# Converting the last four weight chunks in the first layer's first two steps, in half chunks, instead of beside attention

## The chip, the cores and the metric

The kernel runs on one core of a Trainium2 chip, as one launch. The metric is the device time of one execution in microseconds (us). The engines are named as the profile names them: PE is TensorE's matmul, PEld its weight load, DVE is VectorE, ACT is ScalarE, POOL is GpSimd, SP is SyncE, whose queue issues nearly all DMAs here.

## The reference

```python
# attention: 8 batches, 8 heads, 576 tokens, head size 64
scores = scale * np.matmul(q, k.transpose(0, 1, 3, 2))
thresh = np.max(scores, axis=-1, keepdims=True) - tau
scores = np.where(scores >= thresh, scores, -1000000000.0)
attn = np.exp(scores - np.max(scores, axis=-1, keepdims=True))
attn = attn / (np.sum(attn, axis=-1, keepdims=True) + 1e-09)
x = np.matmul(attn, v)                  # then (B,H,S,D) -> (4608 tokens, 512)
# feed-forward
h = np.maximum(x @ w_in, 0.0)           # w_in: 512 x 2048
out = (h * h) @ w_out                   # w_out: 2048 x 512
```

[...]

## The kernel before, in words

**Three stages.** Attention runs in 72 periods, each with two units of 128 queries for two heads. Then come two layers of the feed-forward, each over nine steps of 512 tokens (NSTEP = 9): the first, `hidden_layer`, gives g = relu(x @ w_in)^2, and the second, `output_layer`, gives g @ w_out. Both layers use a two-level fast matrix product that takes seven products where the plain one takes eight, so a step is 7 groups (m in OUTER = 1, 2, 6, 7, 4, 5, 3) of 7 products, 49 products. A product of the first layer is four 128x128 by 128x128 matmuls into one PSUM bank (line 825). The price is sums: of the weights, of x (`prepare_x`, line 774), and of the results.

**A group of the first layer** (`inner`, line 702) makes its products in the order 1, 6, 7, 5, 2, 4, 3 into four banks X, Y, Z, W: X, Y, Z and W get the first four, and X, Z and W are used once more, each accumulating onto what is there. ScalarE copies X out (L737), and VectorE reads Y, Z, W, X, Z, W in that order with an addition each (L125). The sixth product (onto Z) can't begin before VectorE has read the first Z, the seventh (onto W) not before it has read the first W. After each product comes a tick, `also(m, at)`, which issues side work: `convert_out` and `chain_out` first, then in groups three to six (ticks 14 to 40) the sums for the next step's x, `sum_v`, with a ScalarE copy into PSUM (L771) and a VectorE addition (L122). ScalarE also squares finished blocks (L804, L805), and GpSimd makes the rest of the result's sums (L125 on POOL).

**Order.** Everything is under a manual schedule: each engine runs its instructions in the order in which the program issues them, and so does SP's queue with its DMAs.

**The conversion of a weight chunk** (128x512 numbers) has six parts: ScalarE takes the high words' magnitude (`convert1`, L205); GpSimd scales the low words (`convert2`, L212), clamps (`convert3`, L219) and at the end adds (`convert6`, L245); VectorE shifts and merges (`convert4`, L227, and `convert5`, L235). There are 16 chunks of w_in and 16 of w_out. EARLY says how many of w_out's are done beside attention, one chunk started per period: `starts` holds the periods 2 to 33, and a period p is a converting one if p or p - 1 is in `starts`. Such a period uses the order CONVERTING, any other the order PLAIN. In CONVERTING the two reads of the attention output (`values_out`) are ScalarE copies and GpSimd multiplies; in PLAIN they are VectorE multiplies (L644). From the first plain period on, GpSimd also makes the sums of w_in (`sums_step`, at most two in a period before period 60).

**The path of this change.** `convert_out` (line 1057) is called at every tick of the first layer and works on `halves_`, the half chunks of the w_out blocks that are not early, PER = 4 in a step. With EARLY = 16 the list is empty and it does nothing. Converted w_out blocks go to DRAM, where `chain_out` reads them for w_out's own sums; the blocks that stand last in the list are first read there in the third step.

Of the kernel before, what the change touches and what calls it, by code (L numbers as in the profile page):

```python
# [12 lines left out]
U32 = mybir.dt.uint32  # L13
ALU = mybir.AluOpType
AF = mybir.ActivationFunctionType
# [33 lines left out]
def kernel(  # L49
# [25 lines left out]
    nc = tc.nc  # L75
# [82 lines left out]
    def raw_at(m):  # L158
        return RAW.index(m)
# [1 line left out]
    def made_at(m):  # L161
        return 4 + MADE.index(m) if m in MADE else RAW.index(m)

    EARLY = 16
    chunks, out_blocks = [], {}
    for r, c, m_, k_ in blocks(AT_B):
        out_blocks[m_, k_] = moe_w_out[ds(r * BANK, BANK), ts(c, P)].rearrange("(k p) o -> p k o", p=P)
# [2 lines left out]
    blocks_out = [(m, k) for k in RAW for m in RAW]  # L170
    chunks += [(W_OUT, m, k, out_blocks[m, k]) for m, k in blocks_out[:EARLY]]
    is_wide = moe_w_in.dtype != FP32
# [24 lines left out]
    def pick(t, k):  # L197
        return t.rearrange("p (n two) -> p n two", two=2)[:, :, k]
# [7 lines left out]
        parts[m] = (lo, hi, a)  # L206
        raws.pop(m)

    def convert2(m):
        if m in parts:  # L210
            lo = parts[m][0]
            nc.gpsimd.tensor_scalar(out=lo, in0=lo.bitcast(U32), scalar1=2.0**-29, scalar2=None, op0=ALU.mult)  # L212

    def convert3(m):
        if m not in parts:
# [7 lines left out]
    def convert4(m):  # L223
        if m not in parts:
            return
        lo, hi, a = parts[m]
        nc.vector.tensor_scalar(  # L227
            out=a, in0=a, scalar1=3, scalar2=0x3FFFFFFF, op0=ALU.logical_shift_left, op1=ALU.bitwise_and
        )

    def convert5(m):
        if m not in parts:
            return
        lo, hi, a = parts[m]
        nc.vector.scalar_tensor_tensor(  # L235
            out=hi, in0=hi, scalar=-(1 << 30), in1=a, op0=ALU.bitwise_and, op1=ALU.bitwise_or
        )
# [323 lines left out]

    starts = {m + 2: m for m in range(16 + EARLY)}
    X_FIRST = 40
# [44 lines left out]
    def period(p):  # L608
# [63 lines left out]
        def every(key):  # L672
# [7 lines left out]
            "SA": scored_a, "SB": scored_b,  # L680
            "PV": PV, "x": values_out, "xm": given_out,
            "c1": lambda: convert1(begun(p)), "c2": lambda: convert2(begun(p)),
            "c3": lambda: convert3(begun(p)), "c4": lambda: convert4(begun(p - 1)),
            "c5": lambda: convert5(begun(p - 1)), "c6": lambda: convert6(begun(p - 1)),
# [317 lines left out]
    with tc.manual_schedule():  # L1002
# [45 lines left out]
        chain_at, over_at = 26 * BANK, 26 * BANK + 2 * BANK  # L1048
        halves_ = [(m, k, h) for m, k in blocks_out[EARLY:] for h in range(2)]
        chains = [((0, RAW.index(k)), c) for k in RAW for c in range(4)]  # L1050
# [6 lines left out]
        def convert_out(n, tick):  # L1057

            base = X_AT[(n + 1) % 2] + 7 * BANK
            mine = list(enumerate(halves_))[PER * n : PER * (n + 1)]  # L1060
            for j, (i, (m, k, h)) in enumerate(mine):
                place = w_slots[:, raw_at(m), raw_at(k), ds(h * BANK // 2, BANK // 2)]
                raw = arena[:, ds(base + j * BANK, BANK)]
                own = (base - 4 * BANK, base + 4 * BANK, base + 4 * BANK + BANK // 2, over_at)
                a = arena[:, ds(own[j], BANK // 2)]
                key, step = ("out", i), tick - BEGIN - 2 * j
                if tick == 0:
                    src = out_blocks[m, k][:, 2 * h : 2 * h + 2, :]
                    if not is_wide:
                        nc.sync.dma_start(out=two(raw[:, 0 : BANK // 2]), in_=src)  # L1070
                        nc.sync.dma_start(out=place, in_=raw[:, 0 : BANK // 2])
                        continue
                    nc.sync.dma_start(out=two(raw.bitcast(I32)), in_=src.bitcast(I32))
                if not is_wide:
                    continue
                lo, hi = pick(raw.bitcast(I32), 0), pick(raw.bitcast(I32), 1)
                if step == 0:
                    b = b_pool.tile([P, BANK], FP32, tag="b", name="cw")[:, 0 : BANK // 2]
                    nc.scalar.activation(out=b, in_=hi.bitcast(FP32), func=AF.Abs)
                    parts[key] = (lo, hi, b.bitcast(I32))  # L1080
                    convert2(key)
                if step == 2:
                    low, high = (0x38000000, 0x47EFFFFF)
                    b = parts[key][2].bitcast(FP32)
                    nc.vector.tensor_scalar(
                        out=b, in0=b, scalar1=as_float(high), scalar2=as_float(low), op0=ALU.min, op1=ALU.max
                    )
                    convert4(key)
                    convert5(key)
                if step == 5:  # L1090
                    parts.pop(key)
                    nc.gpsimd.tensor_tensor(out=a.bitcast(I32), in0=hi, in1=lo, op=ALU.add)
                if step == 6:
                    nc.sync.dma_start(out=place, in_=a)
# [22 lines left out]
        for n in range(NSTEP):  # L1117
# [15 lines left out]
            def also(m, at):  # L1133
                i = OUTER.index(m)
                convert_out(n, 7 * i + at)
                chain_out(n, 7 * i + at)
                if not last:
                    if 2 <= i <= 5 and at < 6:
                        next(xsums)
                    return  # L1140
                spread(work.get(i, []), at)
                if 7 * i + at > 9:
                    reload(7 * i + at - 10)
# [46 lines left out]
def as_float(bits):  # L1190
    import struct

    return struct.unpack("<f", struct.pack("<I", bits))[0]
# [30 lines left out]
```

## Time and profile before

| | |
|---|---|
| time, median of 3 runs | 1308.91 us (1307.8 to 1309.66) |
| time of the profiled execution | 1308.12 us |
| its span, first to last instruction | 1306.3 us |
| attention (before the first matmul of L825) | 0 to 512.3 us |
| first layer (L825) | 512.3 to 906.5 us |
| second layer (L960) | 906.5 to 1306.3 us |
| busy, share of the span | PE 98%, DVE 77%, POOL 70%, ACT 65% |
| mean granted TensorE clock | 0.998 |

In lines of groups the columns are: line, engine, operation, out<-in, shapes, count, then busy us and mean ns of one, then the engine's idle time before them and what ended it. In lines by windows they are: stretch, its length, busy us of PE, PEld, DVE, ACT and POOL with the number of instructions, granted clock, share of the DMA engines, GB/s. In lines of the timeline they are: start, length, engine, line, operation, count, and in brackets the idle time before.

### The profile page before, as it was taken

The page shows a single profiled execution, that of the slowest core. Times are in us where ns is not written, and L with a number is a line of the kernel's source. Part 1 is how long each engine was busy: PE and PEld are TensorE (multiplying, and loading weights), DVE is VectorE, ACT ScalarE, POOL GpSimd, SP SyncE. Part 2 cuts the span into 40 slices and gives each one's busy share as a digit, 9 for nine tenths or more (in the row PEclk, how much of TensorE's full clock was granted, in tenths as well). Part 3 has the DMA queues.
Part 4 walks back from the last instruction along what each step waited for, and adds up shares of the span by engine and source line. Part 5 has one row for each costly group of instructions (what it writes and reads, how often), then busy time and mean ns, then how long its engine had stood idle before and what let it go on. Part 6 is the DMA issues. An engine that isn't in the chain of part 4 may idle for free.

```text
span 1306.3 us, 47872 instructions
## 1 busy us (share of the span) xinstructions
PE 1284.5 (98%) x19483; PEld 1159.8 (89%) x19483; DVE 1010.8 (77%) x2431; ACT 845.7 (65%) x1498; POOL 916.4 (70%) x1023
## 2 busy tenths in 40 slices
PE   8999999999999999999999999999999999999998
PEld 5777777677777777999999999999999999999998
DVE  5999999999999996877787778777646654665463
ACT  5999999888898985657665766675523432433240
POOL 2777778755555320978897789768777777777775
PEclk9999999999999999999999999999999999999999
DMA  6565666544333313466556665569645234522511
GB/s 153 145 160 140 169 182 188 147 103 104 89 78 79 79 41 80 133 200 218 182 181 194 203 208 164 180 247 393 245 158 162 63 105 158 162 68 96 162 34 33
DMA packets 247035, 192.12 MB, mean 147 GB/s; under 512 B 97184, under 2 KB 195488, under 8 KB 246816
## 3 DMA queue, kind: packets, MB, share of 16 engines
q1 hardware_dynamic: 245504, 188.66, 48.5%
q8 instruction: 153, 2.51, 0.8%
q14 instruction: 66, 0.54, 0.2%
q10 hardware_dynamic: 1312, 0.41, 0.1%
HBM read 116.65 MB, written 72.35 MB: 145 GB/s over the span
## 4 chain that ended last, share of the span: by engine, by line
PE 87%; ACT 5%; DMA 3%; DVE 3%; issue 1%; POOL 1%; SPq 0%; ACTq 0%; DVEq 0%; POOLq 0%
PE po L960 29%; PE ph L825 28%; PE sc L532 11%; PE sc L434 10%; PE pt L380 5%; DVE arena L452 3%; ACT arena L462 2%; PE sc L515 2%; DMA wall<-w 2%; PE sc L398 2%; ACT arena L523 1%; PE sc L380 1%; DMA g<-arena 1%; ACT arena L403 0%; ACT c L771 0%
## 5 line engine op out<-in xcount | busy, mean ns | idle before, releaser
L125 POOL TENSOR_TENSOR arena<-arena 128x512 f32<-128x512 f32 (+1 forms) x314 | 378.1, 1223 | 129.1 <-DVE arena L125 115.1
L960 PE MATMUL po<-wall,arena 128*128 128x128 f32 x3528 | 394.7, 275 | 1.4 <-ACT arena L737 1.4
L960 PEld LDWEIGHTS po<-wall,arena 128*128 128x128 f32 x3528 | 394.3, 192 | 1.8 <-ACT arena L737 1.8
L825 PE MATMUL ph<-arena,wall 128*128 128x128 f32 x3528 | 394.2, 275 | 0.7 <-DVE arena L644 0.7
L825 PEld LDWEIGHTS ph<-arena,wall 128*128 128x128 f32 x3528 | 394.0, 192 | 0.8 <-issue 0.8
L125 DVE TENSOR_TENSOR arena<-ph,arena 128x512 f32<-128x512 f32 x378 | 256.3, 688 | 86.3 <-PE ph L825 63.2
L122 POOL TENSOR_TENSOR arena<-arena 128x128 f32<-128x128 f32 (+2 forms) x314 | 255.4, 814 | 53.8 <-DMA arena<-w 37.6
L125 DVE TENSOR_TENSOR arena<-po,arena 128x128 f32<-128x128 f32 x378 | 108.4, 290 | 168.6 <-PE po L960 164.5
L467 DVE SCALAR_TENSOR_TENSOR arena<-arena 128x576 f32<-128x576 f32 x288 | 237.4, 860 | 1.3 <-POOL arena L459 0.8
L452 DVE TENSOR_SCALAR_CACHE_REDUCE arena<-sc 128x576 f32<-128x576 f32 x288 | 205.0, 747 | 14.6 <-ACT arena L523 4.8
L462 ACT ACTIVATE arena<-arena 128x576 f32<-128x576 f32 x288 | 208.1, 773 | 11.8 <-DVE arena L452 8.5
L771 ACT COPY c<-arena 128x512 f32<-128x512 f32 (+1 forms) x303 | 173.5, 579 | 49.6 <-DVE arena L122 41.7
L532 PEld LDWEIGHTS sc<-arena 64*64 64x64 f32 x5760 | 159.2, 133 | 36.7 <-DVE arena L452 20.2
L532 PE MATMUL sc<-arena 64*64 64x128 f32 (+1 forms) x5760 | 180.8, 262 | 2.7 <-DVE arena L452 1.3
L434 PE MATMUL sc<-arena 64*64 64x64 f32 (+1 forms) x2304 | 176.9, 414 | 6.2 <-ACT arena L403 4.2
L122 DVE TENSOR_TENSOR arena<-arena,c 128x512 f32<-128x512 f32 (+1 forms) x267 | 174.9, 663 | 5.5 <-ACT c L771 4.0
L523 ACT COPY arena<-pt 128x1024 f32<-128x1024 f32 x144 | 146.4, 1017 | 30.5 <-PE pt L380 29.4
L737 ACT COPY arena<-po 128x128 f32<-128x128 f32 x63 | 16.6, 264 | 186.7 <-PE po L960 184.0
L380 PEld LDWEIGHTS pt<-ident,arena 64*128 64x128 f32 x2304 | 83.4, 139 | 39.4 <-ACT arena L523 30.1
L737 ACT COPY arena<-ph 128x512 f32<-128x512 f32 x63 | 36.6, 581 | 123.1 <-PE ph L825 122.5
L434 PEld LDWEIGHTS sc<-arena 64*64 64x64 f32 x2304 | 74.3, 134 | 45.1 <-ACT arena L403 15.1
L380 PE MATMUL pt<-ident,arena 64*128 64x64 f32 x2304 | 102.2, 228 | 2.3 <-ACT arena L523 2.3
(50 smaller groups left out, 922.2 us busy)
## 6 DMA issues: line engine op xcount, KB each, us to landing
g<-arena SPq DMA_DIRECT2D x144, 256.0 KB, 2.6
arena<-g SPq DMA_DIRECT2D x144, 256.0 KB, 4.6
w<-arena SPq DMA_DIRECT2D x60, 256.0 KB, 2.4
wall<-w SPq DMA_DIRECT2D x49, 256.0 KB, 5.2
arena<-w SPq DMA_DIRECT2D x44, 256.0 KB, 3.3
arena<-in_v_dram SPq DMA_DIRECT2D x32, 288.0 KB, 4.0
out_dram<-arena SPq DMA_DIRECT2D x70, 128.0 KB, 2.2
arena<-in_q_dram SPq DMA_DIRECT2D x64, 128.0 KB, 4.0
```

The lines of the kernel that those rows point to most:

```text
L122: e.tensor_tensor(out=out, in0=x, in1=y, op=ALU.subtract)
L125: e.tensor_tensor(out=out, in0=x, in1=y, op=ALU.add)
L380: made = nc.tensor.transpose(pt[:, r, ts(slot, HALF)], of[rows, :], ident[rows, rows])
L434: made = nc.tensor.matmul(sc[at, ds(to, count)], lhs, kT[rows, ds(at_k, count)], start=True, stop=True)
L452: made = nc.vector.tensor_scalar(out=s[:, j, :], in0=sc[:, ds(at, S)], scalar1=1.0, scalar2=None, op0=ALU.mult, op1=ALU.min, accum_out=nmx ...
L462: nc.scalar.activation(out=w[:, :, j, :], in_=of(j), func=AF.Exp, bias=nmx[:, j : j + 1], scale=-1.0)
L467: nc.vector.scalar_tensor_tensor(out=w[:, :, j, :], in0=of(j), scalar=thr[:, j : j + 1], in1=w[:, :, j, :], op0=ALU.is_le, op1=ALU.mult, a ...
L523: touch("weights", nc.scalar.copy(joined(to), whole(pt, 0, count)), at, 2 * BANK, m)
L532: made = nc.tensor.matmul(sc[ds(u * D, D), ds(5 * j * BANK + row, count)], loaded_v[i][rows, (c - (u != j)) % CH, :], wT[m][rows, ds(weigh ...
L771: nc.scalar.copy(c, y)
L825: nc.tensor.matmul(to[:, j, :], W_IN[m, k][:, ts(j, P)], of[k][:, m - 1, :], start=(not more and j == 0), stop=True, skip_group_check=True,)
L960: nc.tensor.matmul(to, g[:, j, :], w[:, j, :], start=(not more and j == 0), stop=(j == 3), skip_group_check=True)
```

## The change

EARLY becomes 12, so that four w_out blocks are left to `convert_out`: eight half chunks, four in each of the first layer's first two steps. Attention's converting periods become 2 to 30, and 31 to 34 become plain. In each of the two steps: at tick 0 SP issues four loads of 256 KB behind the loads of the next x; at ticks 7, 9, 11 and 13 ScalarE takes the magnitude of a half chunk into a PSUM tile (from the pool of two that the x sums use) and, which is new, scales the low words itself; two ticks later VectorE clamps and shifts in that PSUM tile and merges into the SBUF words (three operations of 128x256, each on the result of the one before); three ticks after that GpSimd adds, and at the next tick SP stores 128 KB. PE's instructions are the same in number.

```diff
-    EARLY = 16
+    EARLY = 12
...
-    def convert2(m):
+    def convert2(m, by_scalar=False):
         if m in parts:
             lo = parts[m][0]
-            nc.gpsimd.tensor_scalar(out=lo, in0=lo.bitcast(U32), scalar1=2.0**-29, scalar2=None, op0=ALU.mult)
+            if by_scalar:
+                nc.scalar.activation(out=lo, in_=lo.bitcast(U32), func=AF.Copy, bias=0.0, scale=2.0**-29)
+            else:
+                nc.gpsimd.tensor_scalar(out=lo, in0=lo.bitcast(U32), scalar1=2.0**-29, scalar2=None, op0=ALU.mult)
...
                     nc.scalar.activation(out=b, in_=hi.bitcast(FP32), func=AF.Abs)
                     parts[key] = (lo, hi, b.bitcast(I32))
-                    convert2(key)
+                    convert2(key, True)
```

## The prediction, made before the changed kernel was run

> **What bounds the kernel now.** I read the windows of two attention stretches and of one step of the first layer:
>
> ```profile
> 35.60:256.20 220.60, 216.45 (x5352) 162.16 (x5345) 219.61 (x591) 211.60 (x380) 176.16 (x217) 1.00 0.61 161
> 269.80:500.30 230.50, 227.53 (x6012) 170.98 (x6008) 221.80 (x668) 205.71 (x319) 110.86 (x159) 1.00 0.35 79
> 556.13:599.90 43.77, 43.77 (x394) 43.77 (x393) 34.18 (x55) 28.99 (x53) 36.61 (x46) 1.00 0.62 195
> ```
>
> The first holds converting periods: 31 from reciprocal (L477, one a period) to reciprocal, so 220.60 / 31 = 7.12 us each. The second holds 35 plain ones, 230.50 / 35 = 6.59. VectorE is busy 99.5% of the first and 96% of the second: attention is VectorE's. The third is a first-layer step: PE has no hole, 43.77 / 49 = 0.893 us a product, while VectorE has 9.6 us free. Where that freedom lies is told by VectorE's timeline in the second and third group (m = 2, 6) of the first step:
>
> ```profile
> 520.66 1.52 DVE L125 TENSOR_TENSOR arena<-ph,arena 128x512 f32<-128x512 f32 x2 [1.16 <-PE ph L825]
> 522.38 0.69 DVE L125 TENSOR_TENSOR arena<-ph,arena 128x512 f32<-128x512 f32 x1 [0.20 <-PE ph L825]
> 523.27 0.69 DVE L125 TENSOR_TENSOR arena<-ph,arena 128x512 f32<-128x512 f32 x1 [0.20 <-PE ph L825]
> 524.17 0.69 DVE L125 TENSOR_TENSOR arena<-ph,arena 128x512 f32<-128x512 f32 x1 [0.20 <-PE ph L825]
> 525.06 0.69 DVE L125 TENSOR_TENSOR arena<-ph,arena 128x512 f32<-128x512 f32 x1 [0.20 <-PE ph L825]
> 526.91 0.69 DVE L125 TENSOR_TENSOR arena<-ph,arena 128x512 f32<-128x512 f32 x1 [1.15 <-PE ph L825]
> 527.51 0.68 DVE L122 TENSOR_TENSOR arena<-arena,c 128x512 f32<-128x512 f32 x1
> 528.11 1.51 DVE L125 TENSOR_TENSOR arena<-ph,arena 128x512 f32<-128x512 f32 x2
> ```
>
> The reads follow PE by 0.2 us gaps. Independent operations that are ready start 0.60 apart (526.91, 527.51, 528.11), 0.09 before the one ahead ends; one that uses the result just ahead waits until it has ended and 0.13 more (two in 1.51). Z of group m = 6 is read at 528.11 to 528.79. PE's sixth product there, number 19 counted from 0, starts at 512.36 + 19 x 0.893 = 529.33; PE's first product of the layer began 0.14 after the VectorE read it waited for, so the spare time is 0.40.
>
> **Attention: the gain.** Four periods turn plain: 4 x (7.12 - 6.59) = 2.1 us. VectorE's work says the same: a period loses 422 + 682 ns (rows below) and takes back two multiplies of 285 (L644), 0.53. GpSimd loses 2.04 + 0.61 + 1.48 + 0.73 us a period and does w_in's sums four periods sooner; it is busy 48% of the plain stretch. By single periods the gain is between 1.6 and 2.6.
>
> **First layer, VectorE: the loss.** Three operations of 128x256 per half chunk; the nearest rows:
>
> ```profile
> L411 DVE COPY arena<-sc 128x320 f32<-128x320 f32 x1 | 0.5, 493 | 1.5 <-PE sc L398 1.5
> L125 DVE TENSOR_TENSOR arena<-po,arena 128x128 f32<-128x128 f32 x378 | 108.4, 290 | 168.6 <-PE po L960 164.5
> L235 DVE SCALAR_TENSOR_TENSOR arena<-arena 128x512 int32<-128x512 int32 x32 | 21.8, 682 | 0.0
> L227 DVE TENSOR_SCALAR arena<-arena 128x512 int32<-128x512 int32 x32 | 13.5, 422 | 0.0
> L205 ACT ACTIVATE arena<-arena 128x512 f32<-128x512 f32 x32 | 22.4, 699 | 1.4 <-DMA w<-arena 1.4
> ```
>
> The clamp and the shift work in PSUM, of which before has no row. SBUF's shift takes 422 ns for 512 words, half a nanosecond each; by that rate 256 words take 0.29. The PSUM copy takes 493 for 320, which with 290 for 128 is 1.04 ns each; by that, 256 take 0.42. I take 0.42 for clamp and shift, as their operand is in PSUM like the copy's (ends 0.29 and 0.49), and for the merge 0.42, L235 less 256 x 1.04. With two waits of 0.13 a chain is 1.53 us, and moves VectorE's queue by 1.44.
>
> The Trainium skill (VectorE: DVE Perf Modes, "Why PSUM operands drop a tier") speaks against this change: with a PSUM operand a 32-bit single-source operation loses the double rate that it has in SBUF, so a half chunk there costs as much as a whole one in SBUF. The sum would be the one that follows.
>
> All four chains (ticks 9, 11, 13, 15) stand in VectorE's queue between the Z read of group m = 2 (ends 522.18) and that of m = 6. From 522.18 VectorE now has seven operations, 7 x 0.60 = 4.2, four chains, 5.8, and 0.1 for the tail: Z of m = 6 is read at 532.3, not 528.8. That is 3.5 late, 0.4 of it spare: PE waits 3.1 us per step, some 0.6 of it ahead of the seventh product of m = 2, which needs W, queued behind the first chain. PE has no hole in which to win it back, so it is time.
>
> **First layer, the first chain's data.** Two DMA answers: SP's issues behind the loads of x in the first step, and their time to landing.
>
> ```profile
> 517.29 2.29 SPq L1110 DMA_DIRECT2D arena<-w  x2
> DMA to landing us min/median/max: 5.6/5.8/5.9
> ```
>
> The first new load takes this place and lands at 517.29 + 5.6 = 522.9. ScalarE's magnitude takes 0.48 (L205 less 256 x 0.84), so the first chain starts at 523.4, where VectorE was free at 522.1: 1.3 us more, since VectorE's queue stands behind it (ends: nothing, and 2.2 with the 6.6 us of the slowest w_out load). In the second step the same place is at 560.60 and landed 5.0 later, at 565.6: 566.1 against a Z read that ends at 566.0, 0.2. The other three loads follow at about 0.8 us (256 KB) each, ahead of their chains.
>
> **What is hidden.** ScalarE's 4 x 2 operations of 0.48 are 3.8 us, in the hole before its next copy:
>
> ```profile
> 525.96 0.59 ACT L737 COPY arena<-ph 128x512 f32<-128x512 f32 x1 [5.67 <-PE ph L825]
> ```
>
> Its integer scaling has no row; at GpSimd's rate (L212, 2035 ns for 512, so 1.02) it would be 6.0, about as long as the VectorE queue that it runs beside. GpSimd gets 4 x 0.74 (L245, 1479 for 512), 36.6 + 3.0 of 43.8 us, and no product waits for it; without that cover it would cost up to 3.0 a step. The w_in sums' earlier start costs nothing: no product of attention reads them. SP's g stores and chain loads stand behind four loads, some 3 us; their readers come a step or a layer later. The x sums share the two PSUM tiles: their first copy waits for the third chain, but its addition stands behind the fourth chain anyway.
>
> **Sum.** First step 3.1 + 1.3 = 4.4, second 3.1 + 0.2 = 3.3, attention -2.1: +5.6. On the profiled execution (1308.12; span 1306.3 and 1.8 around it) 1313.7; on the median, 0.8 above it, 1314.5. Cheap end: chains 0.27 shorter, so 2.0 a step, no late data, gain 2.1: +1.9. Dear end: chains 0.2 longer, 3.9 a step, late data 2.2 and 0.2, gain 2.1: +8.1.
>
> **Rivals.** *The clock drops.* PE's waits would be its longest holes. Before shows what a hole can do:
>
> ```profile
> 18.80:22.20 3.40, 1.46 (x24) 0.87 (x28) 3.37 (x10) 3.40 (x8) 0.80 (x1) 1.00 0.80 209
> 22.20:25.60 3.40, 3.40 (x52) 2.40 (x48) 0.60 (x3) 1.61 (x3) 0.00 (x0) 0.50 0.40 90
> ```
>
> A stretch of 3.4 us with PE busy 43% was followed by one at half clock. The wait at the sixth product of m = 6, some 2.6 us in one piece, leaves a stretch of 3.4 us 24 to 62% busy, as it falls. Half clock for 3.4 us costs 1.7: +7.3 with one such stretch, +9.0 with both, 1316.2 to 1317.9. For it: 43% was enough. Against: that stretch was small matmuls, and 70% busy elsewhere cost nothing. The Trainium skill (TensorE: Matmul & The Clock Gate, "HAM oscillation") asks for a hole of about 3.4 us, longer than mine; by that rule the clock holds and my sum stands. The trace above disagrees: its longest hole was 1.47 us.
>
> *VectorE absorbs the chains*, the other side. Free between 522.18 and 526.91 are 4.73 - 4 x 0.60 = 2.3, with the spare 0.4 it is 2.7 a step, so below 0.68 us a chain PE never waits, and attention's gain is all there is: 1308.9 - 2.1 = 1306.8, with the dearest gain 1306.3. For it: VectorE is busy 78% of the step only. Against: it needs chains at under half of my price, below even the cheap end (1.17 less the overlap).
>
> *The change does nothing* because nothing needs converting: L205 and L235 run 32 times, so it does.
>
> **Chances.** My sum with the clock kept 0.45; clock dropping 0.33; absorbed, wholly or nearly (1306.8 to 1310.5), 0.17; worse than all these 0.05. The range 1309.5 to 1318.5 takes in the cheap end, my sum, both clock cases and the dear end. About 0.2%, 2.6 us, is what measuring can tell: faster by more needs over 2.6 from attention and no wait, 0.04; within it (to 1311.5) 0.16; slower 0.80.
>
> **What would show it.** Right: periods 31 to 34 at 6.6 us; in the first two steps PE holes before the seventh product of m = 2 and the sixth of m = 6, ended by VectorE L125; steps of 48 and 47 us, the other seven at 43.77; clamp and shift at 0.42. Wrong: steps still at 43.8, holes ended by ScalarE or GpSimd, a chain of another length, or half clock behind a hole.

## The result, and the profile after

| | before | after |
|---|---|---|
| median of 19 runs each, on the same chip | 1308.53 us | 1312.95 us |
| ratio, 95% interval | | 1.0036 (1.0030 to 1.0042) |
| profiled execution, its span | 1308.12, 1306.3 us | 1311.56, 1309.7 us |
| attention, to the first-layer's first matmul | 512.3 us | 507.6 us |
| first layer / second layer, from the trace | 394.0 / 400.0 us | 402.1 / 400.0 us |

The kernel became slower by 4.4 us by the medians (3.9 to 5.5 by the ratio's interval). In the changed kernel the line numbers behind the two changed functions are 3 higher: L828 is the first layer's matmul, L740 ScalarE's copy, L230 and L238 VectorE's shift and merge; L1088 is the clamp and L1082 the magnitude of a half chunk, L1076 its load, L1113 the load of a chain of w_out's sums.

Windows of the changed kernel: 27 converting periods, 35 plain ones, and the first layer's first three steps (stretch, length, busy us of PE, PEld, DVE, ACT and POOL, clock, DMA share, GB/s).

```profile
35.12:226.24 191.12, 188.53 (x4666) 141.85 (x4658) 191.00 (x515) 184.37 (x334) 153.36 (x189) 1.00 0.61 161
266.12:495.62 229.50, 226.57 (x6004) 170.25 (x6000) 221.41 (x666) 205.57 (x319) 100.00 (x150) 1.00 0.34 80
507.60:555.29 47.69, 44.64 (x392) 44.07 (x393) 37.81 (x65) 26.21 (x50) 31.47 (x41) 1.00 0.56 169
555.29:602.55 47.26, 44.48 (x394) 44.00 (x393) 37.95 (x66) 31.77 (x60) 37.81 (x49) 1.00 0.65 206
602.55:647.00 44.45, 44.11 (x395) 43.92 (x393) 34.61 (x55) 29.02 (x53) 37.29 (x47) 1.00 0.63 197
```

Periods of either kind are nearly what they were (7.12 and 6.59 before, with a few longer single ones among them): 191.12 / 27 = 7.08 and 229.50 / 35 = 6.56. Four have changed kind. The steps are 3.84, 3.49 and 0.67 longer than before's (43.85, 43.77, 43.77), together 8.0. VectorE's busy time in the second step rose by 3.8 (34.18 to 37.95), and the granted clock is 1.00 throughout. The timeline of PE shows where the first two steps grew; in brackets is the hole ahead of each stretch.

```profile
520.74 5.62 PE L828 MATMUL ph<-arena,wall 128*128 128x128 f32 x48 [1.29 <-DVE arena L125]
528.13 38.95 PE L828 MATMUL ph<-arena,wall 128*128 128x128 f32 x344 [1.76 <-DVE arena L125]
568.00 5.62 PE L828 MATMUL ph<-arena,wall 128*128 128x128 f32 x48 [0.93 <-DVE arena L125]
575.48 30.70 PE L828 MATMUL ph<-arena,wall 128*128 128x128 f32 x271 [1.85 <-DVE arena L125]
```

Two holes in each step, before the seventh product of the second group and the sixth of the third (48 matmul records of 5.62 us lie between), each ended by VectorE's read L125. VectorE's timeline in the first step shows the reason; the line below it is from ScalarE's.

```profile
515.98 1.52 DVE L125 TENSOR_TENSOR arena<-ph,arena 128x512 f32<-128x512 f32 x2 [1.16 <-PE ph L828]
518.73 0.43 DVE L1088 TENSOR_SCALAR cw<-cw 128x256 f32<-128x256 f32 x1 [1.23 <-ACT cw L1082]
519.20 0.43 DVE L230 TENSOR_SCALAR cw<-cw 128x256 int32<-128x256 int32 x1
519.67 0.42 DVE L238 SCALAR_TENSOR_TENSOR arena<-arena,cw 128x256 int32<-128x256 int32 x1
520.00 1.28 DVE L125 TENSOR_TENSOR arena<-ph,arena 128x512 f32<-128x512 f32 x2
...
527.39 1.51 DVE L125 TENSOR_TENSOR arena<-ph,arena 128x512 f32<-128x512 f32 x2
```

```profile
518.30 0.40 ACT L1082 ACTIVATE cw<-arena 128x256 f32<-128x256 f32 x1 [2.69 <-DMA arena<-in_moe_w_out_dram]
```

The Y and Z reads of the second group end at 517.50; then VectorE stands 1.23 idle for a magnitude that ScalarE can only make once the raw words have landed (each raw weight is two 32-bit words, high and low, and the loads bring both). Clamp, shift and merge take 0.43, 0.43, 0.42 with only 0.04 between them, and move the queue by 1.27 (518.73 to 520.00). The W read that the seventh product needs starts at 520.00, 2.5 after VectorE was free. From there no read waits for PE: VectorE is full until 527.39, when it reads Z and then W of the third group; the sixth product there waits for that read of Z.

The second step shows something else. First SP's timeline of the changed kernel, then GpSimd's first sum of a chain in the second step, of the changed kernel and (third line) of the kernel before.

```profile
557.59 3.25 SPq L761 DMA_DIRECT2D arena<-xT  x6
560.89 2.00 SPq L1076 DMA_DIRECT2D arena<-in_moe_w_out_dram  x4
562.93 0.64 SPq L1113 DMA_DIRECT2D arena<-w  x1
```

```profile
569.50 2.07 POOL L122 TENSOR_TENSOR arena<-arena 128x128 f32<-128x128 f32 x4 [8.73 <-DMA arena<-w]
```

```profile
565.68 2.06 POOL L122 TENSOR_TENSOR arena<-arena 128x128 f32<-128x128 f32 x4 [5.19 <-DMA arena<-w]
```

The chain load (L1113) stands behind the four late loads and their traffic, and GpSimd waits 8.73 us for it, not 5.19. GpSimd works in order: the result's sums (L125) stand behind the chain's sum. It then ends the step later and VectorE, which adds to what GpSimd has written, waits for it in the third step:

```profile
602.70 0.69 DVE L125 TENSOR_TENSOR arena<-ph,arena 128x512 f32<-128x512 f32 x1 [1.04 <-POOL arena L125]
605.16 1.52 DVE L125 TENSOR_TENSOR arena<-ph,arena 128x512 f32<-128x512 f32 x2 [1.76 <-POOL arena L125]
```

Before, the first of these waits was 0.64 and the second did not exist:

```profile
600.61 0.69 DVE L125 TENSOR_TENSOR arena<-ph,arena 128x512 f32<-128x512 f32 x1 [0.64 <-POOL arena L125]
```

That is the third step's 0.67.

### The profile page after: what moved, and what is told of

It is laid out like the page before. It is cut to its first block, busy times and chain, and to the rows that moved or that the text cites. A ratio compares the mean times of both kernels' runs of the same rounds, so it can differ in the third digit from the quotient of the medians.

```text
span 1309.7 us, 47918 instructions
## 1 busy us (share of the span) xinstructions
PE 1283.4 (98%) x19483; PEld 1158.9 (88%) x19483; DVE 1015.5 (78%) x2455; ACT 846.6 (65%) x1502; POOL 902.7 (69%) x1015
## 4 chain that ended last, share of the span: by engine, by line
PE 51%; DMA 1%; ACT 1%; DVE 0%; issue 0%; POOL 0%; DVEq 0%; POOLq 0%; SPq 0%
PE po L963 29%; PE ph L828 22%; DMA wall<-w 1%; DMA g<-arena 0%; DVE arena L125 0%; ACT arena L808 0%; ACT arena L807 0%; ACT c L774 0%; DVE arena L122 0%; POOL arena L125 0%; ACT arena L740 0%; DVEq L125 0%; DVEq L122 0%; POOLq L125 0%; SPq L1049 0%
## 5 line engine op out<-in xcount | busy, mean ns | idle before, releaser
L125 POOL TENSOR_TENSOR arena<-arena 128x512 f32<-128x512 f32 (+1 forms) x314 | 377.9, 1223 | 126.7 <-DVE arena L125 83.4
L828 PE MATMUL ph<-arena,wall 128*128 128x128 f32 x3528 | 396.1, 275 | 6.9 <-DVE arena L125 6.2
L828 PEld LDWEIGHTS ph<-arena,wall 128*128 128x128 f32 x3528 | 394.6, 192 | 8.3 <-DVE arena L125 5.3
L125 DVE TENSOR_TENSOR arena<-ph,arena 128x512 f32<-128x512 f32 x378 | 255.5, 687 | 83.6 <-PE ph L828 48.2
L125 DVE TENSOR_TENSOR arena<-po,arena 128x128 f32<-128x128 f32 x378 | 108.2, 289 | 168.7 <-PE po L963 164.5
L740 ACT COPY arena<-po 128x128 f32<-128x128 f32 x63 | 16.6, 264 | 186.8 <-PE po L963 184.0
L437 PEld LDWEIGHTS sc<-arena 64*64 64x64 f32 x2304 | 72.9, 134 | 45.1 <-ACT arena L406 16.9
L740 ACT COPY arena<-ph 128x512 f32<-128x512 f32 x63 | 36.4, 578 | 107.9 <-PE ph L828 107.7
```

Source lines behind the costliest of these rows:

```text
L125: e.tensor_tensor(out=out, in0=x, in1=y, op=ALU.add)
L437: made = nc.tensor.matmul(sc[at, ds(to, count)], lhs, kT[rows, ds(at_k, count)], start=True, stop=True)
L828: nc.tensor.matmul(to[:, j, :], W_IN[m, k][:, ts(j, P)], of[k][:, m - 1, :], start=(not more and j == 0), stop=True, skip_group_check=True,)
```

## Experiments

Two theories were to be told apart (the first expectations call them 1 and 2). **A**: VectorE's chains, queued ahead of the reads of Z and W that free PE's banks, and the late data of the first chain, make the whole loss. **B**: the late loads and additions also delay GpSimd, through SP's queue and its own, and GpSimd delays the rest. The table has the first layer's first three steps, each from its first product to the next step's, from one profiled execution of each kernel, and the median and the ratio to the kernel before on the same chip, from all executions.

| run | steps 1, 2, 3 (us) | median (us) | ratio, 95% interval |
|---|---|---|---|
| before | 43.85, 43.77, 43.77 | 1307.7 to 1308.8 | 1 |
| after | 47.69, 47.26, 44.44 | 1312.95 | 1.0036 (1.0030 to 1.0042) |
| e1 transfers only | 43.84, 45.32, 44.73 | 1307.66 | 0.9998 (0.9990 to 1.0007) |
| e2 late and early | 47.18, 47.20, 44.72 | 1315.92 | 1.0063 (1.0050 to 1.0077) |
| e3 no VectorE part | 43.85, 49.36, 45.27 | 1310.41 | 1.0018 (1.0010 to 1.0027) |
| e4 loads first | 46.37, 46.99, 44.70 | 1311.71 | 1.0023 (1.0011 to 1.0036) |
| e5 chain load first too | 46.37, 46.35, 43.79 | 1311.39 | 1.0020 (1.0007 to 1.0032) |
| e6 clamp on GpSimd | 51.55, 51.40, 43.77 | 1320.33 | 1.0089 (1.0074 to 1.0105) |
| e7 same, three a step | 50.24, 49.07, 44.19 | 1315.52 | 1.0055 (1.0042 to 1.0069) |
| e8 transfers, chain first | 43.85, 45.41, 45.26 | 1308.00 | 1.0000 (0.9992 to 1.0009) |
| e9 two a step | 44.09, 45.34, 45.94 | 1324.07 | 1.0130 (1.0115 to 1.0145) |
| e10 three a step | 45.12, 45.44, 45.02 | 1309.31 | 1.0014 (1.0005 to 1.0023) |
| e11 gain alone | 43.85, 43.77, 43.77 | 1305.53 | 0.9980 (0.9971 to 0.9988) |
| e12 stores only | 43.85, 43.77, 43.77 | 1303.99 | 0.9975 (0.9966 to 0.9985) |

**e1, the transfers alone.**

```diff
-                if not is_wide:
-                    continue
+                if step == 6:
+                    nc.sync.dma_start(out=place, in_=wall[:, 0 : BANK // 2])
+                continue
```

> The late half chunks are loaded and 128 KB of other data are stored in their place; all arithmetic of the late conversion is left out. Theory 1 (VectorE's chains stand ahead of the reads of Z and W): the holes of PE go, steps 1 to 3 of the first layer take 43.85, 43.8 and 43.8 us (changed kernel: 47.69, 47.26, 44.45), and what stays is attention's gain, 2.1 us: about 1306.4 against 1308.5. Theory 2 (SP's queue: the chain loads behind the new loads make GpSimd late, and through it ScalarE and VectorE): steps 2 and 3 keep 0.6 to 0.7 us each.

The first step was unharmed, but the second and third cost 1.55 and 0.96 with no arithmetic at all: GpSimd waited 8.65 us for the chain load, as in the changed kernel. So B is real; the transfers are not free.

**e2, the late conversion without attention's gain.**

```diff
-    EARLY = 12
+    EARLY = 16
...
-        halves_ = [(m, k, h) for m, k in blocks_out[EARLY:] for h in range(2)]
+        halves_ = [(m, k, h) for m, k in blocks_out[12:] for h in range(2)]
```

> All 16 w_out chunks are converted beside attention as before, and the last four once more in the first layer: the loss alone, without attention's gain. Theory 1: steps of 47.7, 47.3 and 44.4 us, +8.0 against before, 1316.5. If the changed kernel had more gain in attention than the 2.1 us of the periods, its total (+4.4 to +4.7) and this one differ by that gain: 3.3 to 3.6; if attention gives 2.1, this one is at +6.5 to +6.8 only.

The three steps lose 7.7 in its trace, and the median 7.5. The loss stands by itself.

**e3, without VectorE's three operations**, so that the late chunks stay unfinished.

```diff
-                if step == 2:
-                    low, high = (0x38000000, 0x47EFFFFF)
-                    b = parts[key][2].bitcast(FP32)
-                    nc.vector.tensor_scalar(
...
-                    convert4(key)
-                    convert5(key)
```

> The changed kernel without the three VectorE operations of each late half chunk; loads, ScalarE's two operations, GpSimd's addition and the stores stay. Theory 1: no hole before the products 13 and 19; step 1 at 43.85. Theory 2: GpSimd still gets 4 x 0.61 us and late chain loads, so step 2 keeps about 0.6 us and step 3 about 0.7. A third theory (ScalarE's magnitudes hold up its copies) would keep holes ended by VectorE waiting for ScalarE in step 1. Total by theory 1 and 2 together: -2.1 + 1.3, 1307.7.

In the first step both holes are gone: 43.85. VectorE's chains make that step's loss. The second step, though, grew to 49.36: GpSimd now waits 9.47 us for its chain load, ScalarE's squares wait up to 2.41 for GpSimd, and VectorE 2.12 for ScalarE's copy. A wait was taken away and another, larger one took its place: with VectorE early, GpSimd is the one that is late.

**e4, the four late loads ahead of the loads of x**, issued by a function `load_raw(n)` instead of `convert_out`; and **e5**, which also puts the chain load of the step's first tick ahead of both. The first two added lines are e5's alone, and in e5 `chain_out` no longer issues that load at tick 0:

```diff
             if not last:
+                if PER * n < len(halves_):
+                    chain_out(n, -1)
                 if is_wide:
                     load_raw(n)
                 load_x(n + 1)
```

> The changed kernel with the four late loads issued ahead of the loads of the next x in both steps. If the first chain's data were late (1.23 us of VectorE's wait in step 1, 0.26 in step 2), step 1 falls by 1.2 to 46.5 and step 2 by 0.3 to 47.0, the total by 1.5 to 1311.4. If the lateness only filled a wait that is there anyway, both stay. GpSimd's lateness (step 3: 44.4) should stay, the chain loads are still behind all others.

> Against the kernel with the late loads first, one thing moves: the chain load of the second step stands ahead of the four late loads, not behind them. Theory B (chain load late, so GpSimd's sums late, so ScalarE's squares and copy late, so VectorE late): the second step falls from 46.99 to about 46.3, the third from 44.70 to 43.8, the loss from 6.7 to some 5.1, and VectorE no longer waits for GpSimd at the start of the third step. The first step stays at 46.4, since its chain load comes nowhere near. Theory A (only VectorE's own chains delay the product's reads): all three steps stay as they were, 46.4, 47.0, 44.7. By B the median is some 1310, 1.5 above the kernel before; by A 1311.7.

e4 took 1.32 off the first step and 0.27 off the second: that is the price of the first chain's late data. e5 took a further 0.64 off the second and 0.91 off the third (46.99 to 46.35, 44.70 to 43.79), and nothing off the first: the price of the chain load's place in SP's queue. What is left is 2.52 and 2.58 a step, the four chains themselves. These prices come from single traces: the medians of e4 and e5, 1311.71 and 1311.39, have intervals too wide to tell the two apart.

**e8, the transfers alone with the chain load first** (e1 and the edit of e5 together).

> The run with the transfers alone, no late arithmetic, and the late loads behind the chain load of the second step and ahead of x. Left out: the late conversion itself. Theory B: what the transfers alone cost (45.32 and 44.73 in the second and third step, 2.5 us together) came from the chain load behind them, so both fall to 43.8, the hidden layers to 394.0, and the median to 1305 to 1306. Rival (the transfers cost by their traffic, not by their place in the queue): the second and third step stay at 45 and 44.7, the median at 1307.7.

That failed: 45.41 and 45.26. GpSimd's wait for the first chain load fell to 0.80, but it then waited 3.23 for the second one, and 0.95 and 1.74 for two more. Moving one load ahead moved the wait to the next. The steps are those that the rival gives, by which the transfers cost by their traffic, and the run doesn't rule it out: the second chain load was issued 10.6 us into the step, not 7.7 as before, and also took 6.4 us to land, not 5.4. In e5 VectorE's chains hold up the result's sums anyway, and GpSimd waits 4.10 us for VectorE and only 1.36 each for the first chain load and one later.

**e12, the stores without the loads.** To e1's source:

```diff
-                    nc.sync.dma_start(out=two(raw.bitcast(I32)), in_=src.bitcast(I32))
```

> The transfers-only run without its loads: eight stores of half chunks at their places, no late arithmetic (left out) and no late load. Theory B, with the loads delaying the chain loads behind them: the second and third step fall from 45.3 and 44.7 to 43.8, the median equals that of the gain alone. Rival: the stores, which also stand in SP's queue ahead of chain loads, cost it, and the second and third step stay at 45 and 44.7.

43.77 in the second and third step: it is the loads that delay the chain loads, not the stores.

**e11, attention's gain alone.** This is all that `convert_out` does:

```python
            if n == 0 and 10 <= tick < 18:
                m, k, h = halves_[tick - 10]
                place = w_slots[:, raw_at(m), raw_at(k), ds(h * BANK // 2, BANK // 2)]
                nc.sync.dma_start(out=place, in_=wall[:, 0 : BANK // 2])
```

> Attention without the four late conversions and nothing in their place: left out are the late chunks' loads and arithmetic; eight stores of other data in the first step stand for them. It measures attention's gain by itself. By the periods (four at 7.06 to 7.12 become plain ones at 6.5 to 6.59) the median falls by 2.1 to 2.3, to some 1306.4; by the runs so far (the kernel with the late conversion in both places loses 7.5, this change 4.4) by 3.1 or more, to 1305.5 or less. All steps of the first layer at 43.8.

By the ratios 2.6 us faster (1.6 to 3.8), and e12, whose attention and steps are the same, 3.3 (2.0 to 4.4). Both intervals hold anything from 2.0 to 3.8.

**e6, the clamp taken from VectorE.** To e5's source:

```diff
-                    b = b_pool.tile([P, BANK], FP32, tag="b", name="cw")[:, 0 : BANK // 2]
-                    nc.scalar.activation(out=b, in_=hi.bitcast(FP32), func=AF.Abs)
-                    parts[key] = (lo, hi, b.bitcast(I32))
+                    nc.scalar.activation(out=a, in_=hi.bitcast(FP32), func=AF.Abs)
+                    parts[key] = (lo, hi, a.bitcast(I32))
...
+                if step == 1:
+                    convert3(key)
```

and the clamp on VectorE is dropped. **e7** is e6 with PER = 3 and with the CHAINS of e10 below.

> The kernel with both loads first, and the clamp taken by GpSimd, in SBUF, with the magnitude written there too; VectorE keeps the shift (SBUF, 0.29 by 422 ns for 512 words) and the merge (0.42), a chain that moves its queue by some 0.66 instead of 1.27. Theory A: four chains take 2.6 of VectorE's 2.7 us of freedom between the Z reads of the second and third group, so the two steps fall to 43.9 to 44.3, and the median to some 1306, 2 to 3 under the kernel before. Theory B: GpSimd gets 4 x 0.4 us more a step, its backlog at the step's end grows, and the third step keeps 44.5 or more; the median is then within 1 of the kernel before. If both hold, 1306 to 1307.

> As the one with the clamp on GpSimd, but three half chunks in each of the first two steps and two in the third. Theory A: three chains take 2.0 of the 2.7 us that are free, so no step shows a hole of PE ahead of the third group's products: three steps at 43.8 to 43.9, the median 1305 to 1306. Theory B: GpSimd's additions and the loads are spread over three steps, so no step of the first four is above 44.0; if one is, its hole is released by a VectorE that waited for GpSimd or for ScalarE's copy.

The worst guess of the study: steps of 51.5, not 44. VectorE's and GpSimd's timelines of e6 in the first step (L222 is the clamp on GpSimd, and L1090 its addition):

```profile
526.09 0.54 DVE L230 TENSOR_SCALAR arena<-arena 128x256 int32<-128x256 int32 x1 [1.72 <-POOL arena L222]
526.71 1.31 DVE L238 SCALAR_TENSOR_TENSOR arena<-arena 128x256 int32<-128x256 int32 x1
```

```profile
523.85 1.27 POOL L125 TENSOR_TENSOR arena<-arena 128x512 f32<-128x512 f32 x1 [1.53 <-DVE arena L125]
```

VectorE's chain is shorter but waits for GpSimd's clamp, which is queued behind a result sum, which waits for VectorE's read, which stands behind the chain before. Two queues in order that wait for each other in turn leave PE a hole of 5.16 us (5.30 in the second step). That is not all of the 7.7 that the first step lost. The hole lasted to 531.76, and from 529.74 on the granted clock was 0.50 for 6.83 us (the last three figures are clock, DMA share and GB/s):

```profile
529.74:536.57 6.83, 4.81 (x22) 4.81 (x23) 5.88 (x10) 4.60 (x8) 5.20 (x8) 0.50 0.63 204
```

PE was busy for 4.81 us of it, so 2.4 us went to the clock, which with the hole makes up the loss. The second step has the same (6.83 us at half clock), and e7 has the like: 6.83 and 3.41 us at half clock with holes of 3.28 and 3.43 us.

**e10 and e9, three and two half chunks a step**, with VectorE's operations as they are, from e5:

```diff
-        CHAINS = [49 * n + 6 * c for n in range(NSTEP - 1) for c in range(n == 0, 6)][0 : len(chains)]
+        CHAINS = [49 * n + 6 * c for n in range(NSTEP - 1) for c in range(n == 0, 6)]
+        CHAINS = (CHAINS[0:12] + CHAINS[15:])[0 : len(chains)]
...
-        PER, BEGIN = 4, 7
+        PER, BEGIN = 3, 7
```

This is e10. In e9 PER is 2 and the chains of sums that need the last chunks move back further, so that the steps from the fifth to the eighth get seven chains instead of six:

```diff
+        CHAINS = CHAINS[0:12] + [171 + 6 * c for c in range(4)]
+        CHAINS += [49 * n + 6 * c for n in range(4, 8) for c in range(7)]
```

> Three, three and two half chunks, VectorE's three operations as they were, with the loads and the chain load first. Theory A: three chains are 3.8 us against 2.7 free, so the first two steps show a hole of 1.1 less what the late data add (1.2 to 1.4 over 43.8: 45.0 to 45.3), the third, with two chains, 43.8 to 44.1; the median some 1308, within 1 of the kernel before. Rival: the loss does not go by VectorE's queue but by the number of PSUM operands or of steps touched, and the first two steps stay at 46.4 as with four.

> Two half chunks in each of the first four steps, not four in each of two, with the loads and the chain load first; the sums of w_out that need the last chunks move back to steps 3 to 7, seven a step in the last four. Theory A: two chains take 2 x 1.27 = 2.5 of the 2.7 us that VectorE has free between the Z reads of the second and third group, so PE waits at most for late data: steps of 43.8 to 44.2, no hole over 0.5 us ahead of the third group's sixth product, hidden layers 394 to 395.5, the median 2 to 3 under the kernel before, 1305.5 to 1307. Theory B: the seventh chain of sums per step brings GpSimd to some 38.7 of 43.8 us; if its backlog then reaches ScalarE, steps four to seven (counted from 0) rise over 44 with holes released behind a VectorE that waited for GpSimd, and the gain is lost there.

The first steps are as A says: 46.37, 45.12 and 44.09 with four, three and two chains, 1.25 and 1.03 for one chain less, and two chains fit within 0.24. The later ones are not: 45.02 in e10's third step, which has only two chains, and 45.34 and 45.94 in e9's second and third. VectorE's and PE's timelines of e9 where its third step begins:

```profile
599.36 3.11 DVE L125 TENSOR_TENSOR arena<-ph,arena 128x512 f32<-128x512 f32 x4 [1.77 <-POOL arena L125]
```

```profile
601.73 7.48 PE L828 MATMUL ph<-arena,wall 128*128 128x128 f32 x64 [0.62 <-DVE arena L125]
```

VectorE waits 1.77 for GpSimd's sums of the step before. My reading, not tested by itself: with fewer holes in PE's stream GpSimd no longer has the time to catch up, and it sets the pace. The seven chains a step brought the fifth to eighth steps to 45.5, 47.8, 45.2 and 47.2; the ninth took 45.1, and the second layer 2.8 more than before. No run that converts the late chunks beats the kernel before.

## Why the prediction was right, and where it was not

The sum came out near the result, 1314.5 against 1312.95, and the mechanism was there, but three of its terms were off: the chains 1.1 too dear, what it took as hidden 1.3 too cheap, attention's gain probably about 1 too small. That the first two nearly cancel is luck.

**Attention, predicted 2.1: right for the four periods, but the whole gain was probably larger.** From the third period's reciprocal to the layer's start, before takes 476.6 us and after 472.5; take off single periods that are longer in one execution than in others (before: 0.59, 0.71 and 0.65 at periods 17, 31 and 56; after: 0.19 at 22) and 474.7 and 472.3 remain, a gain of 2.3 to 2.4. But not all of those need be chance. e2, the other kernel with before's attention, takes 476.1, and the twelve with the changed one take 472.4 to 473.7, on average 473.0: 3.4 less than the two. Period 56 is longer by 0.65 and 1.40 in these two traces, and by at most 0.28 in the twelve. Why is open, and two traces are few. The periods 31 to 34 were not all 6.6: the switch of kinds (5.66 and 8.01 us in both kernels) moved there from 35 and 36, and the six together show the gain.

**Where PE waits, and for whom.** Right: the seventh product of the second group and the sixth of the third, ended by VectorE's L125, steps "of 48 and 47 us" at 47.69 and 47.26. That the other seven would stay at 43.77 was wrong for the third, 44.44.

**The chain's price: mis-sized.** "A chain is 1.53 us, and moves VectorE's queue by 1.44": the operations are 0.42 to 0.43 as taken, but the two waits between them are 0.04, not 0.13, and the queue moves by 1.27. With 4 x 0.17 = 0.7 less, the predicted 3.1 a step becomes 2.4; e5 shows 2.52 and 2.58. The choice of 0.42 was right, though its rows, 493 less 290 for 192 words, give 1.06 ns each and not 1.04; that changes 256 words by 0.01 or less. The Trainium skill (VectorE: DVE Perf Modes, "Why PSUM operands drop a tier") says that a PSUM operand holds an fp32 operation to the single rate; this trace shows the same for the int32 shift:

```profile
L230 DVE TENSOR_SCALAR arena<-arena 128x512 int32<-128x512 int32 x28 | 11.7, 417 | 0.0
L230 DVE TENSOR_SCALAR cw<-cw 128x256 int32<-128x256 int32 x8 | 3.5, 432 | 0.3
L1088 DVE TENSOR_SCALAR cw<-cw 128x256 f32<-128x256 f32 x8 | 3.4, 425 | 1.5 <-ACT cw L1082 1.5
L213 ACT ACTIVATE arena<-arena 128x256 int32<-128x256 uint32 x8 | 3.4, 421 | 0.0
```

Half the words in PSUM (second line) take what the whole chunk takes in SBUF (first line); in e6, in SBUF, 256 words took 0.28 where nothing disturbed them. ScalarE's integer scaling, which had no row, is 0.42 against 0.48.

**The first chain's data, 1.3 and 0.2.** Right: e4 puts it at 1.32 and 0.27.

**"What is hidden": the step that failed.** "SP's g stores and chain loads stand behind four loads, some 3 us; their readers come a step or a layer later" is false for the chain loads. The reader is GpSimd six ticks, some 5 us, later, and before already showed it waiting 5.19 for that load; behind the chain's sum in GpSimd's queue stand the result's sums of the running step. "No product waits for it", said of GpSimd's additions, overlooked that VectorE and ScalarE wait for GpSimd's sums, and PE for them. The price is 0.64 in the second step and 0.67 to 0.91 in the third, 1.3 to 1.6 in all, a little more than the chains were overpriced by (3.1 less 2.5, in two steps). So the loss, predicted 7.7, is 8.0.

**The sum against the median.** 8.0 less 3.4 is 4.6, near the 4.4 of the medians; 8.0 less 2.3 would be 5.7, and the interval of the runs ends at 5.5. (In e2, which has before's attention, the 7.7 of the steps and the 7.5 of the medians agree.) The two profiled executions stand 3.3 apart in span: 8.0, less 4.2 from the third period to the layer and 0.5 in the first three periods.

**The clock.** The rival did not come, because its hole did not: 1.76 to 1.85 us, not 2.6. That a longer one can do it shows at the same products in e6 and e7, with their holes of 3.28 to 5.30. Where the border lies is narrowed by windows of two other runs, each cut to the 3.41 us rhythm of the clock's changes: e5 with the hole of 1.76, then e9, where the second layer opens with a hole of 2.68. Whether 2.6 in the first layer would have been enough, no run shows.

```profile
525.35:528.76 3.41, 1.65 (x15) 1.51 (x14) 3.24 (x7) 2.73 (x5) 3.33 (x7) 1.00 0.32 107
528.76:532.18 3.42, 3.42 (x33) 3.42 (x33) 2.69 (x5) 3.36 (x7) 3.42 (x5) 1.00 0.96 307
```

```profile
921.46:924.87 3.41, 1.36 (x12) 1.37 (x13) 1.18 (x4) 0.93 (x4) 3.33 (x4) 1.00 1.04 386
924.87:928.29 3.42, 3.42 (x19) 3.42 (x18) 2.27 (x6) 3.39 (x8) 2.15 (x2) 0.50 1.04 391
```

In these stretches of large matmuls a window with PE busy 48% kept the clock, and one with 40% was followed by 3.4 us at half, as were all four of 2 to 28% in e6 and e7 (by 3.4 or 6.8). The share alone doesn't decide: among the small matmuls at the start, windows of 31% (after) to 66% (e7) were followed by half clock. The Trainium skill (TensorE: Matmul & The Clock Gate, "HAM oscillation") names an idle gap of over about 3.4 us; here 2.68, and 3.28 in e7, were enough.

**VectorE absorbs the chains.** Refuted at four a step, and its threshold nearly right: 2.7 us free were to hold chains of 0.68, and e9's two chains of 1.27 cost its first step 0.24.

## What to carry to other kernels

An engine with 20% of idle time has only what lies ahead of the next operation that someone waits for: count what is queued between two such reads, not the busy share. When a load joins a shared queue, look up the wait of the reader of every load behind it; where before already shows that reader waiting for it (5.19 us here), the new load adds to that wait at once. And moving part of a chain to an engine with idle time helps only if that engine's queue does not itself wait for the engine that is relieved.

## What the runs showed of the hardware

- **Two engines in SBUF.** In e6, while GpSimd was busy, VectorE's merge of 256 words in SBUF took up to 1.31 us against 0.42 at best, and the shift 0.54 against 0.28. That is seen in a few operations, and no run isolates it.
- **The start differs by execution.** In the traces the clock is halved for none, 3.4 or 6.8 us some 20 us after the start, and the second period takes 8.1, 9.3 to 9.7 or 10.2 to 10.4 us accordingly: up to 2 us by which two executions of one kernel differ, whatever is changed in it.
